# Scores of the output factor copied to SBUF before their maximum and exponential

## The chip, the cores and the metric

One NeuronCore of one Trainium2 chip runs one program. The metric is the time of the whole program on the device, in microseconds (us). Engines are named as the profile names them: PE is TensorE (its weight loads are PEld), DVE is VectorE, ACT is ScalarE, POOL is GpSimd, SP is SyncE, which issues the transfers.

## What is computed

Landmark (Nystrom) attention on 4 batches of 8 heads, 576 positions of 64, then two feed-forward layers on the 2304 rows that come out, one with the activation h*cos(h) and one with a leaky rectifier. Three soft maxima stand in the attention; the third, C (landmark queries against all keys), is what the change touches:

```
def sm(a, b):
    s = scale * np.matmul(a, b.transpose(0, 1, 3, 2))
    s = s - np.max(s, axis=-1, keepdims=True)
    e = np.exp(s)
    return e / (np.sum(e, axis=-1, keepdims=True) + 1e-09)
A = sm(q, k_lm)
Bm = sm(q_lm, k_lm)
C = sm(q_lm, k)
...
return (A @ Z @ C @ v).astype(np.float32)
```

## The kernel before, in words

The program has two parts. Up to about 485 us it does attention and the first layer, interleaved: `tick(s)` (128 of them) makes one tile of the first layer's hidden values for 128 hidden units and 288 rows, with six matmuls into a bank "h" (L949), a cosine on ACT and DVE (L954 to L963), and twelve matmuls into four banks "acc" (L976). Between them stand `unit(u)` (8 of them, two per batch, each 4 heads), which makes the soft maxima A and C, `z_path(b)`, which makes the inverse Z, `vprime` (L909), which multiplies Z C v by the first layer's weights, and `convert` (L471, L473, L475), which turns the weights from 64-bit to 32-bit numbers on DVE. From 485 us on the second layer runs (L1235, L1316).

PSUM has eight banks: two "h", two "x", four "acc". The units of batch 0 (m = 0) use "h", "x" and "acc" while no tick runs. The units of batches 1 to 3 (m = 1, u = 2 to 7) have only the two "x" banks for all that they do, and share them with `z_path` and `vprime`.

In such a unit the scores of C come in two pieces of 320 and 256 columns (L670). Both stay in their "x" banks while DVE takes a maximum of each (L685) and one of the two (L687), and until ACT has made the exponentials from there into SBUF with their sums (L692). Then PE transposes the result (L700, L704) and multiplies by v (L715). The scores of A come by the same L670 into "x" again, and DVE transposes them into SBUF (L742).

The order of all work is made by a planner when the program is built (class `Plan`): every operation has a cost, an estimated start and a due time, buffers have so many places, and each engine takes, one after the other, what can start next. Operations that two engines can do are given to the one that is free first. So an edit to one operation moves others on all engines. The lines:

Of the kernel before, what the change touches and what calls it, by code (L numbers as in the profile page):

```python
# [12 lines left out]
AF = mybir.ActivationFunctionType  # L13
ALU = mybir.AluOpType
# [244 lines left out]
def kernel(  # L259
# [12 lines left out]
    nc = tc.nc  # L272
# [63 lines left out]
    def lay(age, at, *items):  # L336
        for tag, n, size in items:
            place[tag] = (age, size, [at + i * size for i in range(n)])
            at += n * size
        return at  # L340

    at = lay(0, 0, ("f", 4, 4 * FW), ("wo", 8, 2048))
    at_va = at
    at = at_a = lay(0, at, ("va", 4, 4096))
    at = at_wi = lay(0, at, ("a", 8, 4 * S))
    at = at_wh = lay(0, at, ("wi", 8, 2048))
    at = at_raw = lay(0, at, ("wt", 4, 1024))
# [9 lines left out]
    def att(m, *items):  # L357
        return [(f"{m}{tag}", n, size) for tag, n, size in items]

    KT, ST = 4 * NR * P, [("cmx", 2, 16), ("cnm", 2, 16), ("csm", 2, 16), ("crs", 2, 16), ("amx", 2, 80), ("asm", 2, 80)]  # L360
    at_z = lay(1, at_1, *att(1, ("kt", 1, KT), ("qt", 2, KT), ("ce", 1, CE), ("at", 2, 4 * S), ("lt", 1, 256), *ST))
    at_0 = lay(0, at_w + 2048, *att(
        0, ("kn", 2, KT), ("qn", 2, KT), ("vn", 2, 4 * RAW), ("kt", 2, KT), ("qt", 2, KT),
        ("ktc", 1, KT), ("qtc", 1, KT), ("ce", 2, CE), ("ls", 4, 512), ("cet", 2, CE), ("at", 2, 4 * S), ("a2", 2, 4 * S),
# [52 lines left out]
    def psb(tag):  # L417
        return g.buf(tag, lambda _: ps.tile([P, 512], F32, tag=tag, name=tag, bufs=g.caps[tag]))
# [32 lines left out]
    def loads(n, fn, dur, r=(), w=(), target=None, after=(), rw=(), hold=()):  # L451
        return op(sp(n), fn, r=r, w=w, rw=rw, target=target, after=after, dma=dur, hold=hold)
# [66 lines left out]
            conv_wo(j)  # L519

    py, Cc = {}, {}
    wt, ah = {}, {}

    def atb(m, tag, shape):
        return sb(f"{m}{tag}", shape)

    def unit(u, tu):
# [37 lines left out]
        def ldv(e):  # L565
            for bb in range(2):
                src = v[b, 4 * c + 2 * bb:4 * c + 2 * bb + 2].rearrange("h (p r) d -> p h r d", r=NR)
                nc.sync.dma_start(out=vv_(vn)[0:64, bb], in_=src[:, :, 0:R0, :])
                nc.sync.dma_start(out=vv_(vn)[64:128, bb, :, 0:R1, :], in_=src[:, :, R0:NR, :])
        loads(4, ldv, 1.64, w=[vn], after=aft)  # L570
        gates["ld"] = aft

        T = {}
# [94 lines left out]
        def scores(dst, ch, which, t, bb, pp):  # L668
            n = 64 * (CH[ch][1] - CH[ch][0])
            nc.tensor.matmul(  # L670
                out=dst.t[64 * bb:64 * bb + 64, 0:n],
                lhsT=kq[pp][:, which, bb].rearrange("p h m -> p (h m)"),
                rhs=t.t[:, CH[ch][0]:CH[ch][1], bb, :],
            )

        sc = pair()
        mx, nm_, sm = atb(m, "cmx", [P, 2]), atb(m, "cnm", [P, 1]), atb(m, "csm", [P, 2])
        for ch in range(2):
            n = (N0, N1)[ch]
# [7 lines left out]
        op(dve(2), lambda e: nc.vector.tensor_reduce(nm_.t, mx.t, axis=AX.X, op=ALU.max, negate=True),  # L687
           r=[mx], w=[nm_])
        ce = atb(m, "ce", [P, R0, 2, 64])
        for ch in range(2):  # L690
            n = (N0, N1)[ch]
            op(("ACT", n / 1200.0 + 0.18), lambda e, ch=ch, n=n: nc.scalar.activation(  # L692
                ce.t[:, 0:n // 64, ch, :], sc[ch].t[:, 0:n].rearrange("p (r s) -> p r s", s=64),
                AF.Exp, bias=nm_.t, accum_out=sm.t[:, ch:ch + 1]), r=[sc[ch], nm_], w=[ce, sm], aset="exp")
# [6 lines left out]
        o1 = op(pe(512, 2), et1, r=[ce], w=[e1, et])  # L701
# [7 lines left out]
        def cv(e):  # L709
# [51 lines left out]
    def z_path(b, tz):  # L761
# [36 lines left out]
        vop(nm_, lambda e: nv.tensor_tensor(bm.t, pbv(), mx.t.to_broadcast([P, n, M]), op=ALU.subtract),  # L798
            r=[pb, mx], w=[bm])
# [582 lines left out]
```

## Time and profile before

| what | us |
|---|---|
| median of 3 runs | 882.39 (881.43 to 885.32) |
| the profiled execution | 881.18 |
| its span in the trace | 879.4 |
| mean granted TensorE clock | 0.984 of full speed |

The page gives the busy time of each engine over the span; since the program has two parts with different limits, the stretches of time are what to read, and within a stretch, which engine waits for which. All rows below come from the profiled execution, which lies 1.2 us below the median of the three runs.

### The profile page before, as it was taken

The numbers are of one execution on the slowest core, as the hardware profiler recorded it, in microseconds if no ns is written. First come the engines' busy times: TensorE is split into PE (matmuls) and PEld (weight loads), VectorE is DVE, ScalarE is ACT, GpSimd is POOL, SyncE is SP. The second block draws the span as 40 slices with busy tenths as digits, with TensorE's granted clock in tenths as the row PEclk, the third lists the DMA queues.
The fourth block names the chain that finished last, engine by engine and source line by source line (L and its number), as shares of the span: only waits on it lengthen the run. The fifth ranks groups of instructions, "written<-read, shape, count | busy, mean of one in ns | idle before, by whom it ended". The sixth has DMA issues, their size and how long they took to land.

```text
span 879.4 us, 15395 instructions
## 1 busy us (share of the span) xinstructions
PE 825.8 (94%) x5681; PEld 726.3 (83%) x5681; DVE 646.4 (74%) x1279; ACT 483.9 (55%) x1118; POOL 198.2 (23%) x220
## 2 busy tenths in 40 slices
PE   5677899999999998999989999999999999999997
PEld 4436789888798887897889888889999999999996
DVE  4989969987896889768998777775665566555563
ACT  4467757777875687667678534443344334333431
POOL 1224511333321332114432222200120012000110
PEclk8989999999999999999999999999999999999999
DMA  8476506775359846666555111140113011310231
GB/s 233 116 215 143 171 26 189 229 178 136 123 159 268 230 119 196 186 182 218 182 185 181 51 48 48 61 132 25 37 61 85 25 37 60 85 37 25 66 115 24
DMA packets 89051, 107.44 MB, mean 122 GB/s; under 512 B 35984, under 2 KB 63120, under 8 KB 88976
## 3 DMA queue, kind: packets, MB, share of 16 engines
q1 hardware_dynamic: 88976, 106.46, 41.2%
q8 instruction: 44, 0.72, 0.3%
q14 instruction: 31, 0.25, 0.1%
HBM read 82.06 MB, written 24.38 MB: 121 GB/s over the span
## 4 chain that ended last, share of the span: by engine, by line
PE 61%; DVE 19%; DMA 10%; issue 3%; ACT 3%; SPq 1%; POOL 1%; DVEq 0%; POOLq 0%; ACTq 0%
PE acc L1316 21%; PE acc L976 10%; PE h L1235 9%; PE x L1235 7%; PE h L949 5%; DMA m<-in_moe_w_in_dram 4%; DMA m<-in_moe_w_out_dram 3%; DVE m L323 3%; DVE m L475 3%; DVE m L473 3%; PE x L909 2%; DMA m<-wi2d 2%; DVE m L471 2%; DVE m L960 2%; DVE m L956 2%
## 5 line engine op out<-in xcount | busy, mean ns | idle before, releaser
L976 PE MATMUL acc<-m,m 128*128 128x288 f32 x1536 | 238.0, 301 | 7.0 <-DVE m L323 3.4
L323 POOL TENSOR_TENSOR m<-m,m 128x288 fp32r<-128x288 f32 (+3 forms) x129 | 126.0, 984 | 459.7 <-ACT m L963 233.5
L976 PEld LDWEIGHTS acc<-m,m 128*128 128x128 f32 x1536 | 213.7, 190 | 18.4 <-issue 7.7
L1316 PE MATMUL acc<-m,m 128*128 128x512 f32 x864 | 207.5, 392 | 0.7 <-DVE m L323 0.4
L323 DVE TENSOR_TENSOR m<-m,m 128x512 fp32r<-128x512 f32 (+4 forms) x271 | 170.3, 651 | 34.9 <-ACT m L1184 9.3
L1316 PEld LDWEIGHTS acc<-m,m 128*128 128x128 f32 x864 | 158.9, 189 | 31.9 <-DVE m L323 0.9
L949 PE MATMUL h<-m,m 128*128 128x288 f32 x768 | 131.8, 307 | 14.9 <-DVE m L960 12.8
L949 PEld LDWEIGHTS h<-m,m 128*128 128x128 f32 x768 | 109.6, 191 | 34.9 <-DVE m L960 19.9
L1304 ACT ACTIVATE m<-m 128x512 fp32r<-128x512 f32 (+1 forms) x80 | 46.3, 588 | 111.5 <-DVE m L1302 109.0
L1235 PE MATMUL h<-m,m 128*128 128x256 f32 x768 | 106.9, 282 | 0.7 <-ACT m L318 0.6
L1235 PEld LDWEIGHTS h<-m,m 128*128 128x128 f32 x768 | 99.7, 189 | 3.6 <-ACT m L318 1.3
L1258 DVE TENSOR_TENSOR m<-h,m 128x512 f32<-128x512 f32 x32 | 22.1, 690 | 81.8 <-ACT m L318 78.9
L1235 PE MATMUL x<-m,m 128*128 128x256 f32 x576 | 80.3, 283 | 1.7 <-ACT m L318 1.7
L963 ACT ACTIVATE m<-m 128x288 fp32r<-128x288 f32 x128 | 55.8, 441 | 40.5 <-DVE m L960 35.4
L1235 PEld LDWEIGHTS x<-m,m 128*128 128x128 f32 x576 | 73.1, 188 | 3.4 <-ACT m L318 1.9
L318 ACT ACTIVATE m<-h 128x256 f32<-128x256 f32 (+2 forms) x93 | 36.8, 396 | 67.2 <-PE h L1235 58.9
L958 ACT ACTIVATE m<-m 128x288 f32<-128x288 f32 x128 | 55.6, 440 | 26.4 <-DVE m L956 26.0
L960 DVE SCALAR_TENSOR_TENSOR m<-m,h 128x288 f32<-128x288 f32 x128 | 56.5, 446 | 15.1 <-ACT m L959 14.8
L1095 ACT ACTIVATE m<-m 128x512 fp32r<-128x512 f32 x68 | 41.4, 628 | 45.0 <-PE h L1235 19.4
L954 ACT ACTIVATE m<-h 128x288 int32<-128x288 f32 x128 | 51.4, 404 | 22.8 <-PE h L949 22.0
L956 DVE SCALAR_TENSOR_TENSOR m<-h,m 128x288 f32<-128x288 f32 x128 | 57.0, 448 | 3.4 <-ACT m L954 3.2
L959 ACT ACTIVATE m<-m 128x288 f32<-128x288 f32 x128 | 55.2, 439 | 2.4
(150 smaller groups left out, 897.5 us busy)
## 6 DMA issues: line engine op xcount, KB each, us to landing
m<-in_moe_w_in_dram SPq DMA_DIRECT2D x32, 512.0 KB, 5.4
m<-in_moe_w_out_dram SPq DMA_DIRECT2D x32, 512.0 KB, 4.4
m<-wi2d SPq DMA_DIRECT2D x56, 256.0 KB, 3.5
m<-w1d SPq DMA_DIRECT2D x32, 256.0 KB, 5.5
y1d<-m SPq DMA_DIRECT2D x24, 288.0 KB, 2.8
out_dram<-m SPq DMA_DIRECT2D x36, 128.0 KB, 2.4
w1d<-m SPq DMA_DIRECT2D x16, 256.0 KB, 5.3
wi2d<-m SPq DMA_DIRECT2D x16, 256.0 KB, 2.9
```

The costliest lines, as they stand in the source:

```text
L323: ENG[e].tensor_tensor(o, a, b, op=ALU.subtract)
L949: nc.tensor.matmul(out=hp.t[:, 0:CW], lhsT=w_[:, js], rhs=x[:, cs], start=(i == 0), stop=(i == 5))
L954: op(act(CW, True), lambda e: nc.scalar.activation(k_.t, hp.t[:, 0:CW], AF.Copy, scale=INV2PI), r=[hp], w=[k_], target=T + 0.8)
L956: op(dve(CW), lambda e: nc.vector.scalar_tensor_tensor(u.t, hp.t[:, 0:CW], INV2PI, k_.t, op0=ALU.mult, op1=ALU.subtract), r=[hp, k_], w=[u])
L958: op(act(CW), lambda e: nc.scalar.activation(u.t, u.t, AF.Sin, scale=math.pi), rw=[u], aset="sin")
L959: op(act(CW), lambda e: nc.scalar.activation(u.t, u.t, AF.Square, scale=math.sqrt(2.0)), rw=[u])
L960: op(dve(CW), lambda e: nc.vector.scalar_tensor_tensor(hc.t, u.t, 1.0, hp.t[:, 0:CW], op0=ALU.subtract, op1=ALU.mult, reverse0=True), r=[h ...
L963: op(act(CW), lambda e: nc.scalar.activation(gh.t, hc.t, AF.Copy), r=[hc], w=[gh, gl])
L976: nc.tensor.matmul(out=yg[o].t[:, 0:CW], lhsT=w_.t[:, sl], rhs=x.t, start=(j == ja and i == 0), stop=(j == jb and i == 2),)
L1235: nc.tensor.matmul(out=rv(k), lhsT=a_.t[:, p, c2, js], rhs=b_.t[:, q_, c2, 0:hw], start=(first and c2 == 0 and i == 0), stop=(c2 == 1 and ...
L1304: op(act(w), lambda e, m_=m_, gh=gh: nc.scalar.activation(gh.t[:, 0:w], m_.t[:, 0:w], AF.Copy), r=[m_], w=[gh, gl])
L1316: nc.tensor.matmul(out=ya[n][t].t, lhsT=gv(x_), rhs=r_.t, start=(st and k == 0), stop=(en and k == 2))
```

## The change

For batches 1 to 3 each piece of the scores is copied to SBUF as soon as it is there, by ACT or DVE, whichever the planner finds free; one maximum over all 576 columns (negated at once) and one exponential over all 576, in place, follow there. The two banks are no longer taken as a pair, neither for C nor, for the first piece, for A. The buffer of C (`1ce`) gets a second place; the room for it comes from `wt`, which goes from four places to two, and from smaller places for the small columns. Batch 0 stays as it was. The dictionary `marks` only keeps names of operations; nothing reads it.

```
-    at = at_raw = lay(0, at, ("wt", 4, 1024))
+    at = at_raw = lay(0, at, ("wt", 2, 1024), ("cex", 1, CE))
...
+    place["1ce"] = (1, CE, place["1ce"][2] + place.pop("cex")[2])
...
-        sc = pair()
-        mx, nm_, sm = atb(m, "cmx", [P, 2]), atb(m, "cnm", [P, 1]), atb(m, "csm", [P, 2])
+        sc = pair() if m == 0 else (psb("x"), psb("x"))
+        mx = None if m else atb(m, "cmx", [P, 2])
+        nm_, sm = atb(m, "cnm", [P, 1]), atb(m, "csm", [P, 2])
+        ce = None
...
+            if m:
+                ce = ce or atb(m, "ce", [P, R0, 2, 64])
+                op(pe(n, 4), cs, r=[kt, kqb[p][1]], w=[sc[ch]])
+                op([act(n, True), dve(n)], lambda e, ch=ch, n=n: copy(
+                    e, ce.t[:, 0:n // 64, ch, :], sc[ch].t[:, 0:n].rearrange("p (r s) -> p r s", s=64)),
+                   r=[sc[ch]], w=[ce])
+                continue
...
+        if m:
+            def ces():
+                return ce.t.rearrange("p r t s -> p (r t s)")[:, 0:S]
+            marks["cn", b, c] = op(dve(S), lambda e: nc.vector.tensor_reduce(
+                nm_.t, ces(), axis=AX.X, op=ALU.max, negate=True), r=[ce], w=[nm_])
+            marks["ce", b, c] = op(("ACT", S / 1200.0 + 0.18), lambda e: nc.scalar.activation(
+                ces(), ces(), AF.Exp, bias=nm_.t, accum_out=sm.t[:, 0:1]), r=[nm_], rw=[ce], w=[sm], aset="exp")
...
+        if m:
+            op(dve(2), lambda e: nc.vector.tensor_scalar_add(rs.t[:, 0:1], sm.t[:, 0:1], 1e-9), r=[sm], w=[rs])
...
-               w=[sa[ch]] if ch else [*sa, at], after=[o1] if ch else [])
+               w=[sa[ch]] if ch else [sa[ch], at] if m else [*sa, at], after=[o1] if ch else [])
```

How the order of the instructions moves is shown at three places. In the rows of the changed kernel the lines of the old steps are 2 to 23 higher (L954 is L977, L956 L979, L960 L983, L963 L986, L670 L672, L700 L719, L704 L723, L715 L734, L976 L999, and L471, L473, L475 are L473, L475, L477).

In these rows m_ and a number is a place in SBUF, and x, h and acc are banks of PSUM.

DVE, first unit of batch 3 (u = 6), from the conversion ahead of the maxima on. Before:

```order
L471 TENSOR_SCALAR m_573<-m_157 128x512
L323 TENSOR_TENSOR m_504<-m_479,m_504 128x288
L473 SCALAR_TENSOR_TENSOR m_573<-m_157,m_573 128x512
L685 TENSOR_REDUCE m_69<-x 128x1 x2
L475 SCALAR_TENSOR_TENSOR m_573<-m_157,m_573 128x512
L687 TENSOR_REDUCE m_69<-m_69 128x1
L956 SCALAR_TENSOR_TENSOR m_479<-h,m_479 128x288
L471 TENSOR_SCALAR m_420<-m_157 128x512
L473 SCALAR_TENSOR_TENSOR m_420<-m_157,m_420 128x512
L475 SCALAR_TENSOR_TENSOR m_420<-m_157,m_420 128x512
L723 SCALAR_TENSOR_TENSOR m_69<-m_69 128x1
L725 RECIPROCAL m_69<-m_69 128x1
```

Now:

```order
L473 TENSOR_SCALAR m_574<-m_157 128x512
L323 TENSOR_TENSOR m_505<-m_480,m_505 128x288
L475 SCALAR_TENSOR_TENSOR m_574<-m_157,m_574 128x512
L477 SCALAR_TENSOR_TENSOR m_574<-m_157,m_574 128x512
L701 TENSOR_REDUCE m_69<-m_175 128x1
L979 SCALAR_TENSOR_TENSOR m_480<-h,m_480 128x288
L473 TENSOR_SCALAR m_421<-m_157 128x512
L764 STREAM_TRANSPOSE m_69<-x 128x320
L475 SCALAR_TENSOR_TENSOR m_421<-m_157,m_421 128x512
L764 STREAM_TRANSPOSE m_69<-x 128x256
L477 SCALAR_TENSOR_TENSOR m_421<-m_157,m_421 128x512
L743 TENSOR_SCALAR m_69<-m_69 128x1
```

The two maxima from the bank x and the small one of the two (L685, L687) are gone, and one maximum from SBUF (L701) stands behind the conversion instead of inside it; the transposes of A's scores (L764) come up ahead of the next conversion's end.

ACT, the same unit, around the exponentials. Before:

```order
L954 ACTIVATE m_479<-h 128x288
L663 ACTIVATE m_69<-m_69 64x2x32 x2
L692 ACT_TABLE_LOAD
L692 ACTIVATE m_175,m_69<-x,m_69 128x5x64
L692 ACTIVATE m_175,m_69<-x,m_69 128x4x64
L954 ACTIVATE m_479<-h 128x288
L958 ACT_TABLE_LOAD
```

Now:

```order
L986 ACTIVATE m_505<-m_480 128x288
L318 ACTIVATE m_175<-x 128x5x64
L318 ACTIVATE m_175<-x 128x4x64
L977 ACTIVATE m_480<-h 128x288
L665 ACTIVATE m_69<-m_69 64x2x32 x2
L703 ACT_TABLE_LOAD
L703 ACTIVATE m_175,m_69<-m_175,m_69 128x576
L977 ACTIVATE m_480<-h 128x288
L981 ACT_TABLE_LOAD
```

Two copies out of x (L318) come first, then the small scalings of the landmarks (L665), and one exponential in place (L703) behind the same table load.

PE, second unit of batch 3 (u = 7), from the transposes of C to its product with v. Before:

```order
L976 MATMUL acc<-m_504,m_1795 128x288 x3
L700 MATMUL x<-m_69,m_175 128x128 x4
L976 MATMUL acc<-m_504,m_1795 128x288 x6
L704 MATMUL x<-m_69,m_175 64x128
L976 MATMUL acc<-m_504,m_1795 128x288 x6
L670 MATMUL x<-m_175,m_69 64x320 x2
L670 MATMUL x<-m_175,m_69 64x256 x2
L976 MATMUL acc<-m_504,m_1795 128x288 x6
L715 MATMUL x<-m_157 32x64 x20
```

Now:

```order
L672 MATMUL x<-m_175,m_69 64x320 x2
L719 MATMUL x<-m_69,m_433 128x128 x4
L999 MATMUL acc<-m_505,m_1791 128x288 x6
L723 MATMUL x<-m_69,m_433 64x128
L999 MATMUL acc<-m_505,m_1791 128x288 x3
L672 MATMUL x<-m_175,m_69 64x256 x2
L999 MATMUL acc<-m_505,m_1791 128x288 x3
L734 MATMUL x<-m_157 32x64 x20
```

The first piece of A's scores (L672, 320 columns) stands ahead of the transposes of C (L719, L723) now, and 12 matmuls into acc instead of 18 stand between these transposes and the product with v (L734).

## Rows read from the trace of the kernel before

**Rows 1.** The page, first part: busy us of each engine, share of span, instructions.
```profile
PE 825.8 (94%) x5681; PEld 726.3 (83%) x5681; DVE 646.4 (74%) x1279; ACT 483.9 (55%) x1118; POOL 198.2 (23%) x220
```

**Rows 2.** Stretches: length; busy (instructions) of PE, PEld, DVE, ACT, POOL; clock; DMA; GB/s.
```profile
50.00:130.00 80.00, 66.31 (x482) 52.81 (x482) 66.92 (x144) 51.03 (x119) 28.61 (x29) 0.94 0.51 137
...
192.00:256.00 64.00, 62.61 (x521) 54.05 (x521) 52.65 (x132) 52.86 (x118) 22.46 (x30) 1.00 0.48 131
...
294.00:366.00 72.00, 68.19 (x551) 58.29 (x552) 62.77 (x142) 54.09 (x125) 24.12 (x32) 1.00 0.56 158
...
485.00:880.00 395.00, 386.18 (x2422) 348.68 (x2420) 242.11 (x415) 149.72 (x323) 52.51 (x51) 0.99 0.19 57
```

**Rows 3.** Waits of PE, 50 to 366 us: total, times, longest.
```profile
PE h L949 <- DVE m L960: 6.7, 11, 3.6
...
PE x L700 <- ACT m L692: 1.5, 1, 1.5
```

**Rows 4.** DVE groups by form, 50 to 366 us: busy, mean ns, idle before.
```profile
L747 DVE TENSOR_REDUCE m<-m 128x18 f32<-128x576 f32 x6 | 4.5, 748 | 0.1
...
L685 DVE TENSOR_REDUCE m<-x 128x1 f32<-128x320 f32 x6 | 2.9, 486 | 0.9 <-PE x L670 0.8
...
L685 DVE TENSOR_REDUCE m<-x 128x1 f32<-128x256 f32 x6 | 2.5, 414 | 0.0
...
L687 DVE TENSOR_REDUCE m<-m 128x1 f32<-128x2 f32 x6 | 0.9, 143 | 0.0
```

**Rows 5.** The same view, operations that either engine can do (last row: 0 to 485).
```profile
L320 DVE COPY m<-x 128x384 f32<-128x384 f32 x5 | 2.8, 555 | 2.3 <-PE x L594 2.2
...
L320 DVE COPY m<-x 128x512 f32<-128x512 f32 x2 | 1.4, 681 | 0.0
...
L320 DVE COPY m<-m 32x64 f32<-32x64 f32 x6 | 1.1, 181 | 0.1
...
L323 DVE TENSOR_TENSOR m<-m,m 128x288 fp32r<-128x288 f32 x60 | 34.9, 587 | 7.0 <-ACT m L963 5.6
```

**Rows 6.** ACT groups by form, 50 to 366 us.
```profile
L318 ACT ACTIVATE m<-x 128x384 f32<-128x384 f32 x28 | 12.9, 488 | 2.7 <-PE x L594 2.5
...
L749 ACT ACTIVATE m<-m 128x576 f32<-128x576 f32 x6 | 4.1, 683 | 0.1
...
L692 ACT ACTIVATE m<-x,m 128x320 f32<-128x320 f32 x6 | 3.2, 527 | 0.1
L692 ACT ACTIVATE m<-x,m 128x256 f32<-128x256 f32 x6 | 2.8, 467 | 0.0
```

**Rows 7.** First unit of batch 3: chain (first row), DVE and ACT in time order.
```profile
304.55 1.12 PE x L670 x8
...
306.62 0.82 DVE L685 TENSOR_REDUCE m<-x 128x1 f32<-128x320 f32 x2
...
306.70 0.41 ACT L954 ACTIVATE m<-h 128x288 int32<-128x288 f32 x1 [2.06 <-PE h L949]
...
307.52 1.28 ACT L692 ACT_TABLE_LOAD   x1
308.81 0.53 ACT L692 ACTIVATE m<-x,m 128x320 f32<-128x320 f32 x1
...
309.69 0.20 ACT L692 ACTIVATION_READ_ACCUMULATOR m<-x,m 128x1 f32 x1
```

**Rows 8.** Waits of DVE, 50 to 366 us: total, times, longest.
```profile
DVE m L471 <- DMA m<-in_moe_w_in_dram: 7.1, 6, 2.4
...
DVE m L742 <- PE x L670: 2.3, 3, 1.2
...
DVE m L750 <- ACT m L749: 1.5, 1, 1.5
...
DVE m L723 <- ACT m L692: 1.3, 2, 0.6
...
DVE m L685 <- PE x L670: 0.8, 2, 0.5
```

More of the change, by code (lines that the diff above doesn't have):

```diff
@@ L340, in lay @@
         return at
+    CE = 4 * R0 * P
     at = lay(0, 0, ("f", 4, 4 * FW), ("wo", 8, 2048))
@@ L346 @@
     at = at_wh = lay(0, at, ("wi", 8, 2048))
-    at = at_raw = lay(0, at, ("wt", 4, 1024))
-    CE = 4 * R0 * P
+    at = at_raw = lay(0, at, ("wt", 2, 1024), ("cex", 1, CE))
     at = lay(0, at, ("raw", 3, 4 * RAW))
@@ L360 @@
     KT, ST = 4 * NR * P, [("cmx", 2, 16), ("cnm", 2, 16), ("csm", 2, 16), ("crs", 2, 16), ("amx", 2, 80), ("asm", 2, 80)]
-    at_z = lay(1, at_1, *att(1, ("kt", 1, KT), ("qt", 2, KT), ("ce", 1, CE), ("at", 2, 4 * S), ("lt", 1, 256), *ST))
+    ST1 = [("cnm", 2, 8), ("csm", 2, 8), ("crs", 2, 8), ("amx", 2, 72), ("asm", 2, 72)]
+    at_z = lay(1, at_1, *att(1, ("kt", 1, KT), ("qt", 2, KT), ("ce", 1, CE), ("at", 2, 4 * S), ("lt", 1, 256), *ST1))
     at_0 = lay(0, at_w + 2048, *att(
@@ L521 @@
     py, Cc = {}, {}
-    wt, ah = {}, {}
+    wt, ah, marks = {}, {}, {}
     def atb(m, tag, shape):
@@ L569, in ldv @@
                 nc.sync.dma_start(out=vv_(vn)[64:128, bb, :, 0:R1, :], in_=src[:, :, R0:NR, :])
-        loads(4, ldv, 1.64, w=[vn], after=aft)
+        marks["vl", b, c] = loads(4, ldv, 1.64, w=[vn], after=aft)
         gates["ld"] = aft
@@ L686, in unit @@
                r=[sc[ch]], w=[mx])
[L687 to L694, printed above, removed]
+        if m:
[5 more added lines that the diff above has]
+                ces(), ces(), AF.Exp, bias=nm_.t, accum_out=sm.t[:, 0:1]), r=[nm_], rw=[ce], w=[sm], aset="exp")
+        else:
+            op(dve(2), lambda e: nc.vector.tensor_reduce(nm_.t, mx.t, axis=AX.X, op=ALU.max, negate=True),
+               r=[mx], w=[nm_])
+            ce = atb(m, "ce", [P, R0, 2, 64])
+            for ch in range(2):
+                n = (N0, N1)[ch]
+                op(("ACT", n / 1200.0 + 0.18), lambda e, ch=ch, n=n: nc.scalar.activation(
+                    ce.t[:, 0:n // 64, ch, :], sc[ch].t[:, 0:n].rearrange("p (r s) -> p r s", s=64),
+                    AF.Exp, bias=nm_.t, accum_out=sm.t[:, ch:ch + 1]), r=[sc[ch], nm_], w=[ce, sm], aset="exp")
         e1, e2 = bank(0), bank(1)
@@ L700, in et1 @@
                 nc.tensor.transpose(e1.t[:, r * P:(r + 1) * P], ce.t[:, r].rearrange("p t s -> p (t s)"), ident)
-        o1 = op(pe(512, 2), et1, r=[ce], w=[e1, et])
+        o1 = marks["et", b, c] = op(pe(512, 2), et1, r=[ce], w=[e1, et])
         op([act(512), dve(512)], lambda e: copy(e, et.t[:, 0:R1].rearrange("p r m -> p (r m)"), e1.t),
@@ L722, in unit @@
         rs = atb(m, "crs", [P, 2])
-        op(dve(2), lambda e: nc.vector.scalar_tensor_tensor(
-            rs.t[:, 0:1], sm.t[:, 0:1], 1e-9, sm.t[:, 1:2], op0=ALU.add, op1=ALU.add), r=[sm], w=[rs])
+        if m:
+            op(dve(2), lambda e: nc.vector.tensor_scalar_add(rs.t[:, 0:1], sm.t[:, 0:1], 1e-9), r=[sm], w=[rs])
+        else:
+            op(dve(2), lambda e: nc.vector.scalar_tensor_tensor(
+                rs.t[:, 0:1], sm.t[:, 0:1], 1e-9, sm.t[:, 1:2], op0=ALU.add, op1=ALU.add), r=[sm], w=[rs])
         op(dve(2), lambda e: nc.vector.reciprocal(rs.t[:, 1:2], rs.t[:, 0:1]), rw=[rs])
@@ L747, in unit @@
         op(dve(S), lambda e, mxa=mxa, at=at: nc.vector.reduce_max(mxa.t, at.t, axis=AX.X), r=[at], w=[mxa])
-        op(tt, lambda e, mxa=mxa, at=at: sub(e, at.t, at.t, mxa.t.to_broadcast([P, NBK, M])), r=[mxa], rw=[at])
-        op(act(S), lambda e, at=at: nc.scalar.activation(at.t, at.t, AF.Exp), rw=[at], aset="exp")
+        marks["as", b, c] = op(tt, lambda e, mxa=mxa, at=at: sub(
+            e, at.t, at.t, mxa.t.to_broadcast([P, NBK, M])), r=[mxa], rw=[at])
+        marks["ae", b, c] = op(act(S), lambda e, at=at: nc.scalar.activation(at.t, at.t, AF.Exp), rw=[at], aset="exp")
         op(dve(S), lambda e, sma=sma, at=at: nc.vector.reduce_sum(sma.t, at.t, axis=AX.X), r=[at], w=[sma])
@@ L797, in z_path @@
         vop(nm_, lambda e: nv.reduce_max(mx.t, pbv(), axis=AX.X), r=[pb], w=[mx])
-        vop(nm_, lambda e: nv.tensor_tensor(bm.t, pbv(), mx.t.to_broadcast([P, n, M]), op=ALU.subtract),
-            r=[pb, mx], w=[bm])
+        marks["zs", b] = op(dve(nm_), lambda e: nv.tensor_tensor(
+            bm.t, pbv(), mx.t.to_broadcast([P, n, M]), op=ALU.subtract), r=[pb, mx], w=[bm])
         op(act(nm_), lambda e: nc.scalar.activation(bm.t, bm.t, AF.Exp, scale=8.0), rw=[bm], aset="exp")
```

## The prediction

> **What bounds the kernel now.** I read four views, from coarse to fine. The page's first part [rows 1] shows PE busy for 94% of the span; that alone would say that work of DVE and ACT is free. The table by stretches [rows 2] says otherwise, and it is the view to read here. From 485 us on PE is busy 386.18 of 395 us: nothing there waits for the units, and the change alters nothing in it. The units that the change touches stand in three earlier stretches: batch 1 at 50 to 130 us, batch 2 at 192 to 256, batch 3 at 294 to 366. In each, PE loses time (13.7, 1.4 and 3.8 us idle), and DVE is busy 66.92 of 80, 52.65 of 64 and 62.77 of 72 us: 82 to 87%, which leaves little for waits in one queue that takes its work in order. So I take DVE as what sets the pace there. The waits of PE over 50 to 366 us [rows 3] fit: the longest is PE at a tick's first matmuls for L960, a DVE step (6.7 us in 11 waits). Of the changed steps PE has waited for the exponential (L692) once, 1.5 us. No wait of PE names a bank; a bank that is late shows as a wait for whoever reads it last.
>
> **DVE's work.** Six units change. Out go twelve maxima from PSUM: 2.9 us for the six of 320 columns, 2.5 for the six of 256; and six small maxima of the two, 0.9 [rows 4]. In come six maxima over 576 columns from SBUF. The trace has that operation in another place: L747, a maximum over 576 fp32 columns from SBUF, 4.5 us for six. The new one has one output column in place of 18; I take the same price. The small addition after it (one operand in place of two) takes the place of L723 and is priced as it. Of the twelve copies the order gives eleven to ACT and one of 256 columns to DVE; between a maximum over as many PSUM columns (0.41 us [rows 4]) and a copy of 384 (0.56 [rows 5]) I take 0.43, near the first, which has the same size. Sum: 4.5 + 0.4 - 5.4 - 0.9 = -1.4 us.
>
> The planner also shifts work that either engine can do. Counted over both orders DVE loses five copies of 32x64, one of 128x384 and one subtraction of 128x288, and gains two copies of 128x512: by rows 5, -0.91 - 0.56 - 0.59 + 1.36 = -0.7 us. (One small copy goes and one small scaling comes; I set them against each other.) DVE has 2.1 us less to do in all. With DVE busy 85% of these stretches, 0.85 x 2.1 = 1.8 us of it lies on the path. Bounds: 0, if what is saved only lengthens DVE's waits, and -2.1.
>
> The Trainium skill speaks against this part: Perfetto Trace Analysis, Optimizing Scalar/DVE Operations, says that long operations pay where the engine is saturated, and that where it only causes bubbles elsewhere, broken-up work may finish sooner. By the same section's overheads of an instruction on DVE (some 125 ns on PSUM, 60 on SBUF) I would estimate that one maximum saves 2 x 125 - 60 = 190 ns against two, 1.1 us over six units; rows 4 give 0.9. Which half of the rule holds hangs on whether DVE is saturated; 85% is nearer to saturated, so by it the sum stands, and by its other half the first rival below comes true.
>
> **ACT's work.** Out: twelve exponentials, 3.2 + 2.8 us, with a read of the accumulator of 0.20 behind each, 2.4 us [rows 6, 7]. In: six exponentials over 576 columns at 0.68 (L749's price) with a read each, 5.3 us, and eleven copies of 256 or 320 columns, for which I take 0.44, somewhat under the 0.49 that 384 take, 4.8 us. That is +1.7 us; the table loads stay as many. ACT is busy 51 to 54 us in stretches of 64 to 80 [rows 2], so I cost this at nothing: the cover is DVE, which has more to do. If the cover were gone, at most +1.7.
>
> **The chain inside a unit.** In the first unit of batch 3 the scores begin at 304.55, the first maximum starts at 306.62, the last exponential's read ends at 309.89 [rows 7]: both banks are held for over 5 us. Of this the changed work is 0.82 (maxima), 0.14 for the small one [rows 4], and 1.08 (exponentials); the table load of 1.28 overlaps part of it and stays. Now: the copies end some 0.5 us after the last score, the maximum takes 0.75, the exponential with its read 0.88. That is 2.0 before and 2.1 now. The chain does not get shorter; what gets shorter is the time for which the banks are held, from 5 us to about 1.5. PE has no matmul more or less. The second place of `1ce` takes a wait away that no row shows; the two places of `wt` that go cost nothing, since a batch's tile is used up (last by its L909) long before the batch after next needs the place. No transfer is added; SP's order shifts by a few loads around the units, and I cost that at nothing, with the longest wait of DVE for such weights, 2.4 us [rows 8], as the bound either way.
>
> **Sum.** -1.8 us against the profiled execution's 881.18. That execution lies 1.2 us below the median of the runs, and a median is what will be measured, so I set the sum against 882.4: **880.6 us**. About 0.5%, 4.4 us, is what a measurement of this kernel can tell from no change; the forecast is below that.
>
> **Rivals.**
>
> 1. *A new wait on ACT.* Until now DVE took a maximum as soon as PE had a piece ready. Now PE hands to ACT and ACT to DVE, and in DVE's queue the long maximum stands ahead of ticks' steps (L960) for which PE waits. If DVE gets there before the copies have landed, it stands still for a copy (0.4 us) and for what ACT has ahead of it: between nothing and a table load of 1.28 [rows 7]. Taking the middle, 1.1 us for each of six units: +6.6, with the 1.8 less that is +4.8, **887.2 us**. For it: DVE was already there too early for scores in two maxima and three transposes (0.8 and 2.3 us [rows 8]). Against it: the order now puts the maximum behind a whole conversion, and ACT stood idle for 2.1 us just ahead of the unit's exponentials [rows 7]. It decides if DVE waits for L318 ahead of L701 by over 4 us in total.
>
> 2. *Early banks set the units free.* With the banks held for 1.5 us, A's scores come earlier (in the second unit of batch 3 their first piece has moved ahead of C's transposes), and DVE's waits inside the units go: L742 for L670 2.3 us, L750 for L749 1.5, L723 for L692 1.3, L685 for L670 0.8 [rows 8], 5.9 us in all. With the 1.8 that is -7.7: **874.7 us**. Against it: these are waits in a queue that has other work, and what stands behind moves up to the next wait (that for the weights' transfers is the next, 7.1 us [rows 8]). The Trainium skill is on this rival's side: PSUM — Partial Sum Buffer, Summary: rules for kernel authors, says to evacuate promptly because the memory is tight. Rows 3 show little waiting for it.
>
> 3. *It does not do what it says.* The copies stand in queues in order; where they wait there, the banks come free no sooner, and only the 1.8 us remains, eaten by ACT's +1.7: **882.4 us**.
>
> **How the numbers follow.** Forecast 0.43, first rival 0.22, second 0.25, third 0.10. The forecast's bounds and the third rival lie within 4.4 us of 882.4 but for tails, which the reshuffled order gives both: 0.03 to faster, 0.03 to slower. So faster 0.28, same 0.47, slower 0.25. The range takes in the forecast with its bounds, about half of the second rival (874.7 lies just outside, 0.13 left out) and two thirds of the first (0.07 left out): 875.0 to 888.0.
>
> **What would show it.** Right: in the three stretches DVE's busy sum falls by about 2 us (182.3 now [rows 2]) and ACT's rises by 1 to 2; L701 reads 0.75 us; PE's matmuls from 485 us on are as long as before; the tick waits of PE for L960 stay near 6.7 us. The first rival shows as DVE waits for L318 and longer PE waits for L960, the second as missing waits at L742, L750 and L723 and a second layer that starts 6 us sooner. Wrong is the forecast if the start of the second layer moves by over 4 us either way, above all if it moves though DVE's sum in the stretches is the one forecast: then the order, and not the work, has decided.

## The result: slower by 0.7%

The changed kernel takes 889.04 us (median of 13 runs, 885.53 to 891.97) against 882.39 (13 runs, 879.70 to 886.28): a ratio of 1.0067, with a 95% interval of 1.0045 to 1.0089. The forecast was 880.6, with 875.0 to 888.0 as its range. The two profiled executions, 885.60 and 881.18 us, lie 4.4 us apart and not 6.7, since that of the changed kernel is one of its shorter runs; the tables below are made from them, so they hold some two thirds of the loss.

First the work. The page of the changed kernel, its first part:

```profile
PE 826.2 (93%) x5681; PEld 726.4 (82%) x5681; DVE 645.0 (73%) x1263; ACT 487.4 (55%) x1121; POOL 196.3 (22%) x221
```

Against [rows 1] PE is the same, DVE has 1.4 us less, ACT 3.5 more. The same stretches as in [rows 2], with PE, PEld, DVE, ACT and POOL in this order:

```profile
50.00:130.00 80.00, 66.82 (x477) 53.90 (x477) 66.72 (x142) 54.16 (x120) 24.37 (x26) 0.89 0.51 137
192.00:256.00 64.00, 62.65 (x523) 53.58 (x522) 51.34 (x126) 50.86 (x112) 19.82 (x28) 1.00 0.48 132
294.00:366.00 72.00, 70.09 (x569) 59.76 (x566) 61.40 (x138) 57.74 (x135) 25.67 (x33) 1.00 0.63 173
```

DVE's sum is 179.5 us, 2.9 less than the 182.3 of before. ACT's is 162.8, 4.8 more than the 158.0 of before, where 1 to 2 were forecast. The changed kernel is late in these stretches, so they do not hold quite the same work; cut at the same ticks (below), DVE's sum falls by 2.3 us and ACT's rises by 3.3. Either way DVE has less to do. The groups by form, DVE and then ACT, 50 to 370 us, answer to [rows 4, 6]:

```profile
L701 DVE TENSOR_REDUCE m<-m 128x1 f32<-128x576 f32 x6 | 4.5, 749 | 1.2 <-ACT m L318 1.0
...
L703 ACT ACTIVATE m<-m,m 128x576 f32<-128x576 f32 x6 | 4.7, 776 | 0.1
```

The new maximum takes 749 ns, the price taken for it was 748; the exponential in place takes 776 and not 680. The first unit of batch 3, chain, DVE and ACT in time order, as in [rows 7]:

```profile
311.86 0.76 PE L672 MATMUL x<-m,m 128*64 128x320 f32 x4
...
312.67 0.44 ACT L318 ACTIVATE m<-x 128x320 f32<-128x320 f32 x1 [0.26 <-PE x L672]
...
313.14 0.65 PE L672 MATMUL x<-m,m 128*64 128x256 f32 x4
...
313.84 0.39 ACT L318 ACTIVATE m<-x 128x256 f32<-128x256 f32 x1 [0.73 <-PE x L672]
...
314.45 0.74 DVE L701 TENSOR_REDUCE m<-m 128x1 f32<-128x576 f32 x1
```

From the first score to the end of its copy a bank is held for 1.25 us (311.86 to 313.11), the other for 1.1. Before, the first was held for 4.8 us (304.55 to the end of its exponential, 308.81 plus 0.53) and the second, taken together with it, for over 5. The change does what it says.

**Where the time goes.** In the trace a tick begins with the first of six matmuls of L949 (L972 now); there are 768 of them, six for each of 128 ticks. Between the same ticks the two kernels do nearly the same work, so I cut both traces at ticks 0, 22, 40, 64, 88 and 127. Before:

```profile
47.00:143.40 96.40, 81.82 (x587) 66.40 (x586) 81.71 (x174) 63.37 (x151) 29.69 (x30) 0.95 0.49 134
143.40:191.90 48.50, 46.76 (x326) 42.12 (x325) 46.67 (x90) 35.12 (x90) 15.64 (x13) 1.00 0.68 205
191.90:276.30 84.40, 82.84 (x664) 72.49 (x664) 68.43 (x166) 65.52 (x149) 26.18 (x34) 1.00 0.57 164
276.30:366.60 90.30, 85.33 (x663) 72.71 (x663) 75.01 (x169) 63.87 (x148) 25.73 (x34) 1.00 0.64 176
366.60:478.90 112.30, 106.04 (x736) 97.07 (x735) 93.09 (x175) 79.54 (x202) 37.73 (x39) 0.98 0.62 205
```

Now:

```profile
47.20:143.90 96.70, 83.23 (x581) 67.37 (x580) 80.87 (x172) 66.08 (x152) 26.52 (x28) 0.91 0.48 132
143.90:198.20 54.30, 48.59 (x338) 43.61 (x337) 48.88 (x89) 36.64 (x93) 17.88 (x16) 1.00 0.67 200
198.20:286.10 87.90, 84.33 (x660) 73.12 (x659) 69.95 (x162) 63.87 (x146) 24.91 (x33) 0.98 0.50 148
286.10:370.60 84.50, 82.59 (x660) 71.66 (x659) 70.64 (x156) 64.99 (x152) 27.53 (x35) 1.00 0.67 183
370.60:485.00 114.40, 105.70 (x740) 96.25 (x740) 92.31 (x177) 79.18 (x201) 37.32 (x39) 1.00 0.63 204
```

The first window holds batch 1's units and is 0.3 us longer; the fourth, with those of batch 3, is 5.8 shorter. The loss is in the second (+5.8), the third (+3.5) and the last (+2.1); a second trace of the changed kernel (e9 below) has +6.0, +1.6 and +2.9 there. The second is the one to look at first: no changed step runs between ticks 22 and 40, and it is where DVE was fullest, 46.67 of 48.5 us. There DVE has one instruction fewer, yet is busy 2.2 us longer and PE waits more. PE's and DVE's waits there, before:

```profile
PE h L949 <- DVE m L960: 1.1, 3, 0.6
PE h L949 <- DVE m L912: 0.5, 1, 0.5
...
DVE m L471 <- DMA m<-in_moe_w_in_dram: 1.3, 2, 0.8
DVE m L471 <- DMA m<-in_moe_w_out_dram: 0.4, 1, 0.4
```

and now:

```profile
PE h L972 <- DVE m L983: 5.7, 6, 1.6
...
DVE m L473 <- DMA m<-in_moe_w_in_dram: 2.2, 3, 1.4
DVE m L473 <- DMA m<-in_moe_w_out_dram: 1.8, 1, 1.8
```

One place shows how. DVE of the changed kernel at tick 28, and PE behind it:

```profile
159.57 0.68 DVE L477 SCALAR_TENSOR_TENSOR m<-m,m 128x512 int32<-128x512 int32 x1
162.07 0.43 DVE L473 TENSOR_SCALAR m<-m 128x512 int32<-128x512 int32 x1 [1.82 <-DMA m<-in_moe_w_out_dram]
162.53 0.69 DVE L475 SCALAR_TENSOR_TENSOR m<-m,m 128x512 int32<-128x512 int32 x1
163.14 0.45 DVE L979 SCALAR_TENSOR_TENSOR m<-h,m 128x288 f32<-128x288 f32 x1
163.51 0.44 DVE L983 SCALAR_TENSOR_TENSOR m<-m,h 128x288 f32<-128x288 f32 x1
...
164.01 1.07 PE L972 MATMUL h<-m,m 128*128 128x288 f32 x6 [1.61 <-DVE m L983]
```

A weight conversion's first two steps (L473, L475) stand ahead of the steps of two ticks. Its weights have not landed, DVE stands still for 1.82 us, L983 comes late, and PE waits 1.61 us for it. In the kernel before the same conversion stands behind the steps of both ticks, and DVE waits 0.38 us for it:

```profile
159.30 0.44 DVE L960 SCALAR_TENSOR_TENSOR m<-m,h 128x288 f32<-128x288 f32 x1
159.66 0.44 DVE L956 SCALAR_TENSOR_TENSOR m<-h,m 128x288 f32<-128x288 f32 x1
160.49 0.43 DVE L471 TENSOR_SCALAR m<-m 128x512 int32<-128x512 int32 x1 [0.38 <-DMA m<-in_moe_w_out_dram]
```

None of these is a changed step: behind batch 1, where the changed steps are planned otherwise, the planner puts the rest elsewhere too.

The third window has the same picture at one place, with the clock behind it. DVE and PE in time order, then the stretch from 278 us:

```profile
275.17 0.43 DVE L473 TENSOR_SCALAR m<-m 128x512 int32<-128x512 int32 x1 [2.70 <-DMA m<-in_moe_w_in_dram]
...
276.02 1.06 PE L972 MATMUL h<-m,m 128*128 128x288 f32 x6 [2.11 <-DVE m L983]
...
278.31 1.64 PE L972 MATMUL h<-m,m 128*128 128x288 f32 x6
...
278.00:280.00 2.00, 2.00 (x11) 2.00 (x10) 1.13 (x3) 0.90 (x3) 0.00 (x0) 0.50 1.01 350
```

DVE stands still for 2.70 us for weights ahead of L983, and PE waits 2.11 us for that step. Right behind this pause the granted clock falls from 1.00 to 0.72 of full speed in the mean of 276 to 282 us, with 0.50, the lower of its two levels (1.2 GHz), at 278 to 280; six matmuls of L972 take 1.64 us there and 1.06 just before. The wait and the clock (6 us at 0.72, some 1.7 us by my estimate) together are about the 3.5 us that this window loses. In e9, where it loses 1.6, the clock of the window reads 1.00.

### The profile page after: what moved, and what is told of

Its sections match the earlier page's. It is cut to its first block, busy times and chain, and to the rows that moved or that the text cites. A ratio compares the mean times of both kernels' runs of the same rounds, so it can differ in the third digit from the quotient of the medians.

```text
span 883.8 us, 15379 instructions
## 1 busy us (share of the span) xinstructions
PE 826.2 (93%) x5681; PEld 726.4 (82%) x5681; DVE 645.0 (73%) x1263; ACT 487.4 (55%) x1121; POOL 196.3 (22%) x221
## 4 chain that ended last, share of the span: by engine, by line
PE 64%; DVE 16%; DMA 9%; ACT 4%; issue 4%; SPq 1%; POOL 1%; DVEq 0%; POOLq 0%; ACTq 0%
PE acc L1339 20%; PE acc L999 12%; PE h L1258 9%; PE x L1258 7%; PE h L972 6%; DMA m<-in_moe_w_in_dram 4%; DVE m L323 3%; DVE m L475 2%; DMA m<-in_moe_w_out_dram 2%; PE x L932 2%; DVE m L477 2%; DMA m<-wi2d 2%; DVE m L473 2%; DVE m L979 2%; DVE m L983 1%
## 5 line engine op out<-in xcount | busy, mean ns | idle before, releaser
L999 PE MATMUL acc<-m,m 128*128 128x288 f32 x1536 | 237.6, 301 | 4.4 <-ACT m L457 1.9
L999 PEld LDWEIGHTS acc<-m,m 128*128 128x128 f32 x1536 | 214.3, 190 | 15.4 <-issue 7.6
L323 DVE TENSOR_TENSOR m<-m,m 128x512 fp32r<-128x512 f32 (+4 forms) x270 | 167.7, 643 | 34.3 <-ACT m L1207 9.0
L972 PE MATMUL h<-m,m 128*128 128x288 f32 x768 | 134.5, 311 | 17.5 <-DVE m L983 16.4
L972 PEld LDWEIGHTS h<-m,m 128*128 128x128 f32 x768 | 111.4, 194 | 38.8 <-DVE m L983 22.4
L986 ACT ACTIVATE m<-m 128x288 fp32r<-128x288 f32 x128 | 56.1, 441 | 46.8 <-DVE m L983 43.9
L318 ACT ACTIVATE m<-h 128x256 f32<-128x256 f32 (+2 forms) x93 | 36.9, 397 | 66.2 <-PE h L1258 58.1
L983 DVE SCALAR_TENSOR_TENSOR m<-m,h 128x288 f32<-128x288 f32 x128 | 57.0, 446 | 15.0 <-ACT m L982 14.9
L977 ACT ACTIVATE m<-h 128x288 int32<-128x288 f32 x128 | 51.7, 404 | 24.6 <-PE h L972 23.8
L979 DVE SCALAR_TENSOR_TENSOR m<-h,m 128x288 f32<-128x288 f32 x128 | 57.3, 449 | 6.0 <-ACT m L977 5.6
```

The costliest lines, as they stand in the source:

```text
L972: nc.tensor.matmul(out=hp.t[:, 0:CW], lhsT=w_[:, js], rhs=x[:, cs], start=(i == 0), stop=(i == 5))
L977: op(act(CW, True), lambda e: nc.scalar.activation(k_.t, hp.t[:, 0:CW], AF.Copy, scale=INV2PI), r=[hp], w=[k_], target=T + 0.8)
L979: op(dve(CW), lambda e: nc.vector.scalar_tensor_tensor(u.t, hp.t[:, 0:CW], INV2PI, k_.t, op0=ALU.mult, op1=ALU.subtract), r=[hp, k_], w=[u])
L983: op(dve(CW), lambda e: nc.vector.scalar_tensor_tensor(hc.t, u.t, 1.0, hp.t[:, 0:CW], op0=ALU.subtract, op1=ALU.mult, reverse0=True), r=[h ...
L986: op(act(CW), lambda e: nc.scalar.activation(gh.t, hc.t, AF.Copy), r=[hc], w=[gh, gl])
L999: nc.tensor.matmul(out=yg[o].t[:, 0:CW], lhsT=w_.t[:, sl], rhs=x.t, start=(j == ja and i == 0), stop=(j == jb and i == 2),)
```

## The experiments

**Theory "order"**: the changed steps are worth about the forecast's sum, and the reshuffled queues cost the rest. **Theory "steps"**: copies, a longer chain through ACT, and steps in place cost it, and the order only shows it. To part them I made the planner's order something that can be carried over: each step has a name (its context and its number there) that both kernels share, and the list of steps with their engines, as the planner put them out, is written into the kernel and followed.

```diff
+        todo = {}
+        for e, rank, key in ORDER:
+            todo.setdefault(e, []).append((rank, key))
         while left:
             best = None
-            for e, lst in ready.items():
+            if any(todo.values()):
...
+                            sl = None if o is None else slots(o)
+                            if sl is None:
+                                continue
...
+                            if best is None or rank < best[0]:
+                                best = (rank, d, o, s, e)
...
+                todo[best[4]].remove((best[0], best[2].key[2]))
+            for e, lst in () if best else ready.items():
```

In a kernel with this list the lines behind it are some 270 higher than in the changed kernel (L1244 is its L972, L949 in the kernel before; L1255 its L983, L960 before). The list holds a step's place and its engine together, so the runs do not part these two; "order" below means both. All medians and ratios stand in the table at the end of this section.

**e1: the new steps in the old order.** Seven steps of a unit become six where they stood:

```diff
-scores0 max0 scores1 max1 small_max exp0 exp1
+scores0 copy0 scores1 copy1 max exp
```

> The changed steps (copies, one maximum, one exponential, the new places in SBUF, banks singly) in the order of the kernel before on all five queues; a copy stands where a maximum stood, the long maximum where the small one stood, the exponential where the first one stood. Theory 'order' (the planner's reshuffled queues cost the 6 us, the steps themselves are worth about what the sum said): 879 to 883 us, ratio 0.996 to 1.001. Theory 'steps' (the copies and the chain through ACT and DVE cost it): 887 to 890, ratio 1.006 or more.

Measured: 880.28 us, ratio 0.9975 (0.9957 to 0.9993). "Steps" is out: in the old order the new steps are faster than the old ones by 2.2 us (0.6 to 3.8), and the forecast's sum was 1.8. The new places in SBUF are in this kernel too, so they do not cost the loss either. Most of the waits that the second rival wanted to see gone are still there; in DVE's waits, 50 to 366 us, the transpose of A's scores (L1036 here) and the sum behind the exponential of A (L1045) read

```profile
DVE m L1036 <- PE x L944: 2.0, 3, 1.2
DVE m L1045 <- ACT m L1044: 1.5, 1, 1.5
```

against 2.3 and 1.5 in [rows 8].

**e2: the old steps in the new order**, the same in the other direction.

> The converse: the old steps (two maxima, a small one, two exponentials, banks in pairs, old places) in the order of the changed kernel; 16 pairs of neighbours among some 4,160 steps swap where a bank is not yet free. Theory 'order': 887 to 891 us, ratio 1.005 to 1.010, with the second layer late as in the changed kernel. Theory 'steps': 881 to 884.

Measured: 893.98 us, ratio 1.0122 (1.0095 to 1.0149), beyond what either theory said. The order costs 1.2% with the old steps; with the new ones the step from 0.9975 to 1.0067 is 0.9% (0.75% to the 1.0050 of e9). In this order too the new steps are the better ones, 1.0067 against 1.0122. But it was planned for the new steps: here 6.1 of the 12.5 us are lost before tick 22, among the units of batch 1, where the changed kernel loses 0.5. So e2 shows that this order is a bad one for the old steps, not that it loses at the same places.

**e3: the changed kernel with SP's queue in the old order.**

> The changed kernel with SP's queue (all transfers) in the order of the kernel before; the other four queues as in the changed kernel. If the loss comes from the order of the transfers (DVE's waits for weights between the units 4.0 us against 1.8): 882 to 885 us, ratio 1.000 to 1.003. If it comes from what stands where on DVE and PE: 887 to 890, ratio 1.005 or more. Theory 'steps': 887 to 890 too.

Measured: 899.1 us, ratio 1.0197 (1.0163 to 1.0231), a miss: beyond the times of both branches. In ticks 22 to 40 it loses 6.2 us, as much as the changed kernel, so the loss there is not due to the order of the transfers alone. Some 11.4 more are lost in ticks 52 to 58, where one row of DVE's waits (251 to 280 us; L744 is L471) has the reason:

```profile
DVE m L744 <- DMA m<-in_moe_w_in_dram: 9.1, 2, 5.2
```

Here an order of transfers belongs to the order of the queue that uses them; half of one and half of the other is worse than either.

**e4: the old order up to tick 64, the changed kernel's from there.**

```diff
-ORDER: changed kernel, ticks 0 to 128 and the second layer
+ORDER: kernel before to tick 64; changed kernel behind it
```

> The changed steps, in the order of the kernel before up to tick 64 (233 us of the plan, 250 us of the trace), and from there in the order of the changed kernel. Theory 'order', with the loss in ticks 8 to 64 (+9.8 us at tick 64) and a gain in batch 3 (-5.9 from tick 64 to tick 88): 876 to 881 us, ratio 0.993 to 0.999. If the loss is one that follows whatever stands before, or the gain was only the catching up of a late PE: 882 to 886. Theory 'steps': 887 to 890.

Measured: 878.85 us, ratio 0.9961 (0.9941 to 0.9981), inside the range of "order" with a place. The trace has it nearly as expected: -1.4 us at tick 40, -0.9 at 64, -5.9 at 88, so a gain of 5.1 from 64 to 88 where 5.9 was expected. That e4 beats e1 is not shown, the intervals overlap.

**e5: that kernel with ticks 22 to 40 in the changed order**, the window by itself.

> The fourth run's kernel (changed steps, old order to tick 64) with one window more in the changed order: ticks 22 to 40 of every queue. If that window's order costs its 5.8 us by itself: ratio to the kernel before 1.001 to 1.005 (0.9961 without it), with PE waiting for L960's step 5 us there and tick 40 some 4 to 6 us later than in the fourth run. If the 5.8 us hang on what stood before the window, or are given back behind it: ratio 0.995 to 0.998.

Measured: 0.9983 (0.9963 to 1.0003), 0.2% over e4 and between the two branches; the intervals of the two overlap, so by the times alone no cost of the window is shown. In the trace it costs 3.8 us (from -0.9 at tick 22 to +2.9 at tick 40, against nothing in e4), PE waits 4.5 us for L983's step there, and e5 is 3.3 us behind e4 at tick 127. So by one trace of each the window's order does cost by itself, but some 3 to 4 us rather than 5.8. Ticks 22 to 40 of e4, then of e5:

```profile
142.00:190.50 48.50, 46.52 (x326) 42.11 (x325) 46.50 (x90) 35.06 (x90) 15.53 (x13) 1.00 0.69 202
142.46:194.82 52.36, 47.69 (x333) 42.83 (x332) 49.16 (x89) 36.40 (x93) 17.50 (x16) 1.00 0.71 206
```

DVE is busy 2.7 us longer with one instruction fewer, as it is in the changed kernel (2.2 us), while POOL has 16 instructions in place of 13. DVE's waits for weights are only 1.4 us here, less than the 1.7 of the kernel before. So late weights are not needed for the loss; DVE's longer work, on which the last section has more, is the greater part of it in e5.

**e10: the converse, the changed kernel with ticks 22 to 40 in the old order.**

> The changed kernel with one window, ticks 22 to 40 of every queue, in the order of the kernel before; all else as changed. If the 5.8 us of that window are its order's own: 3 to 6 us under the ninth run of the same chip, ratio 0.999 to 1.004, tick 40 at most 1.5 us later than before. If they hang on the state in which the window is reached: within 2 us of the ninth run.

Measured: 885.75 us, 2.6 under the changed kernel's 888.36 on the same chip (ratio 1.0025, 1.0006 to 1.0044): between the two branches, and the intervals of the two ratios overlap. In the trace the gain is whole up to tick 37: +1.2 us against the +6.4 of e9. Then most of it goes, for a reason that is new. PE's waits, 145 to 196 us:

```profile
PE x L868 <- DMA m<-in_q_dram: 2.3, 1, 2.3
PE h L1244 <- DVE m L1255: 1.1, 1, 1.1
```

The waits for L983's step are down to 1.1, as in the kernel before, and PE comes to the transposes of q of batch 2 before q has landed: tick 40 is at +4.5.

**e6: four DVE steps moved up**, L983 of ticks 22, 27, 31 and 35, each ahead of the last one or two steps of a conversion. At tick 27:

```diff
+L983 (tick 27)
 L473 (conversion 20)
 L475 (conversion 20)
 L979 (tick 28)
-L983 (tick 27)
```

> The changed kernel with four DVE steps moved up and nothing else: in ticks 22, 27, 31 and 35 the step of L983 goes ahead of the one or two steps of a weight conversion that stood before it. If PE's waits for L983 in ticks 22 to 40 (5.7 us in 6) come from those steps of conversion standing ahead: waits of PE there under 3 us, ratio to the kernel before 1.002 to 1.005 in place of 1.0067. If DVE is short of time there as a whole (it then only waits for the same weights a step later): 1.006 to 1.008.

Measured: ratio 1.0032 (1.0009 to 1.0054), but on another chip than the changed kernel's 1.0067; **e9** ran the changed kernel again to settle that.

> The changed kernel once more, unaltered, beside the next three on one chip, and with a second trace. The sixth run's ratio (1.0032 with four moves) was taken on another chip than the changed kernel's 1.0067. If the four moves gained what their ratio says: this comes out at 1.005 or more, with PE waiting longer for L983 in ticks 22 to 40 than the sixth run's 5.0 us. If the sixth run's trace is right (tick 40 only 0.5 us earlier) and the rest is a difference between chips: 1.002 to 1.005.

Measured: 888.36 us, 1.0050 (1.0031 to 1.0069), and PE's waits for L983 there are 4.6 us. The two intervals overlap, so no gain of the four moves is shown. The trace of e6 shows what became of the waits; those of PE and DVE, 143.5 to 197.7 us (L1241, L1252 and L742 are L972, L983 and L473, and L1251 is the step of ACT ahead of L983):

```profile
PE h L1241 <- DVE m L1252: 4.9, 8, 1.5
...
DVE m L1252 <- ACT m L1251: 2.5, 3, 1.3
...
DVE m L742 <- DMA m<-in_moe_w_in_dram: 0.9, 2, 0.5
```

DVE's waits for weights fall from 4.0 to 0.9 us, and a wait for ACT takes their place: at its new place L983 comes before ACT has its operand ready. My guess that the conversions in front of L983 are the whole cause is wrong; here, where DVE has 46.67 of 48.5 us to do, the steps moved away from one wait landed in the next. Which of the moved steps of the window would have to go back stays open.

**e7, e11, e12: a reshuffle with nothing of the change in it.** The kernel before, where only the planner's price of a DVE step is altered:

```diff
-        return ("DVE", n / 960.0 + 0.07)
+        return ("DVE", n / 960.0 + 0.071)
```

and 0.069 and 0.072. This moves 241, 184 and 242 steps on DVE, where the change moves 244.

> The kernel before, nothing of the change in it; the planner's price of a DVE step is 0.001 us higher, which moves 241 steps on DVE and 16 on SP against the order before (the change moves 244 and 19). It measures what a reshuffle costs by itself. Theory 'order', with orders differing by chance about a tuned one: outside 0.997 to 1.003, slower likelier, about 1.005 to 1.015. If a reshuffle of this size is harmless by itself: 0.998 to 1.002.

> The kernel before with the planner's price of a DVE step 0.001 us lower: 184 steps move on DVE, 11 on SP. A second draw of a reshuffle without the change, after 1.0011 for the first. If draws spread by half a per cent or more: outside 0.998 to 1.002; if a reshuffle of this size is worth less than the change's order (e2: 1.012 with the old steps): 0.998 to 1.004.

> The same with the price 0.002 us higher: 242 steps move on DVE, 15 on SP. A third draw; as for the eleventh run.

Measured: 1.0011 (0.9991 to 1.0030), 1.0070 (1.0041 to 1.0098) and 1.0059 (1.0035 to 1.0082). Two of three cost as much as the change. The first costs nothing that can be measured and so falls into the branch that spoke against "order": a reshuffle of this size can be harmless. With the change's own order (e2) that is four other orders for the same steps, and none is better than the one before.

**e8: the best windows put together**, with the new steps: old order to tick 64, new in 64 to 88, old in 88 to 128, new in the second layer.

> The changed steps; order of the kernel before to tick 64, of the changed kernel in ticks 64 to 88 (which gained 4.5 us in the fourth run), of the kernel before in ticks 88 to 128 (the fourth run lost 2.2 there), of the changed kernel in the second layer (gained 1.5). If windows add up: 876 to 878 us, ratio 0.992 to 0.995. If what a window gains hangs on what follows it: like the fourth run, 0.996, or worse.

Measured: 878.95 us, ratio 0.9939 (0.9916 to 0.9962): faster than both kernels, with the ratio in the first branch and the median just above it. That it also beats e4 is not shown, the intervals overlap.

The whole on one page: medians, ratios, and the start of a tick against that of the kernel before, in us (one trace each; the last column is the end of the span).

| kernel | median us | ratio | 22 | 40 | 64 | 88 | 127 | end |
|---|---|---|---|---|---|---|---|---|
| before, from the span's start | 882.39 | | 143.4 | 191.9 | 276.3 | 366.6 | 478.9 | 879.4 |
| changed | 889.04 | 1.0067 | +0.5 | +6.3 | +9.8 | +3.9 | +6.1 | +4.4 |
| e9, changed again | 888.36 | 1.0050 | +0.9 | +6.9 | +8.5 | +2.8 | +5.7 | +5.6 |
| e1, new steps, old order | 880.28 | 0.9975 | +0.8 | +1.0 | +0.7 | +1.5 | +1.5 | +1.3 |
| e2, old steps, new order | 893.98 | 1.0122 | +6.1 | +10.4 | +14.3 | +10.9 | +14.1 | +12.5 |
| e3, old order on SP alone | 899.10 | 1.0197 | +3.9 | +10.1 | +20.1 | +17.9 | +21.4 | +21.2 |
| e4, old order to tick 64 | 878.85 | 0.9961 | -1.4 | -1.4 | -0.9 | -5.9 | -3.7 | -5.2 |
| e5, e4 with new 22 to 40 | 882.23 | 0.9983 | -0.9 | +2.9 | +3.1 | -1.7 | -0.4 | -0.6 |
| e10, changed with old 22 to 40 | 885.75 | 1.0025 | +1.7 | +4.5 | +7.3 | +2.9 | +5.6 | +5.5 |
| e6, changed, four moves | 886.39 | 1.0032 | +0.2 | +5.8 | +9.3 | +3.4 | +5.7 | +4.0 |
| e7, before, price 0.071 | 884.75 | 1.0011 | +1.7 | +3.0 | +0.7 | +1.1 | +2.3 | +0.6 |
| e11, before, price 0.069 | 889.92 | 1.0070 | +3.9 | +6.8 | +8.3 | +5.8 | +7.7 | +7.7 |
| e12, before, price 0.072 | 888.82 | 1.0059 | +3.8 | +5.1 | +5.9 | +5.6 | +6.4 | +6.3 |
| e8, best windows | 878.95 | 0.9939 | +1.1 | +1.0 | +1.5 | -1.8 | -0.3 | -2.1 |

One trace of each is read here, and two traces of the changed kernel (its own and e9's) differ by up to 1.4 us at one tick; differences of that size in the table mean nothing. The spread is understated by this pair: single runs of the changed kernel lie between 885.53 and 891.97 us, and the execution traced can lie well off the median, 2.2 us above it in e1 and 2.9 below it in e4. So e1's +1.3 at the end stands beside a median that is lower than before, and the ratios decide. They are of several runs each, against those of the kernel before on the same chip.

## Why the prediction was wrong

**The sum is not contradicted.** -1.4 us for DVE's changed steps and -1.8 on the path was the forecast, the latter with a third from the planner's shifts; with the order held (e1), and so without these shifts, the steps gain 2.2 us (0.6 to 3.8). The new maximum reads what L747 reads, and the bank's hold falls to 1.25 us where about 1.5 was said. That the gain comes the way the sum says is not shown: in e1's trace DVE is busy 641.5 us against 646.4, and 3.9 of these 4.9 us are in the three steps of the conversions (133.2 against 137.1), which the edit does not touch. ACT's rise in the stretches was undersized (+4.8 against +1 to 2, +3.3 by ticks; of this 0.6 us is the exponential's 776 ns in place of 680), and it cost nothing that e1 shows.

**The step that failed is the planner's shifts.** The prediction priced the reshuffle by which steps change their engine (-0.7 us) and SP's order at nothing, with 2.4 us as the bound. The runs show 6.6 to 8 us in place of -0.7: with the same new steps the ratio goes from 0.9975 in the old order to 1.0050 (e9) and 1.0067 in that of the change. Two things were missing. What stands ahead of what was not priced: the bound was a single wait of one queue, where ticks 22 to 40 alone have four waits for weights, six waits of PE and the steps behind them. And a step was taken at the same price whatever its neighbours: with three more subtractions on POOL there, DVE is busy 2.2 us longer (2.7 in e5). How the 6.6 to 8 us divide between the two is not shown, since every list carries places and engines together.

**The stretches left out the fullest one.** I read [rows 2] only where changed steps stand, and took DVE's 82 to 87% there for the sign that DVE sets the pace. Between them, from tick 22 to tick 40, DVE was 96% busy (46.67 of 48.5) with PE waiting 1.6 us in all: the tightest of the five windows, with no changed step in it, and every reshuffle in the table that begins before it passes through it. From tick 22 to 40 the changed order loses 5.8, e2 4.3, e3 6.2, and the three nudges (e7, e11, e12) 1.2, 2.9 and 1.3; kernels with the old order there lose at most 0.2 up to tick 37. It is not the only place, though: e2 and the nudges lose more before tick 22 (6.1, 1.7, 3.9 and 3.8), and putting the window back (e10) returns 2.6 us of the change's loss. That the rest falls before tick 64 is shown by e4; where, the trace alone says (the third window above).

**The rivals.** The first was right in sign and near in size (887.2) by luck, for a reason that is not there: DVE waits for L318 ahead of L701 once, 1.0 us, where over 4 was asked. In the changed kernel's waits of DVE, 50 to 366 us:

```profile
DVE m L473 <- DMA m<-in_moe_w_in_dram: 8.0, 7, 2.7
...
DVE m L773 <- ACT m L772: 4.0, 3, 1.6
...
DVE m L764 <- PE x L672: 1.1, 3, 0.5
DVE m L701 <- ACT m L318: 1.0, 1, 1.0
```

The waits for the exponential of A (L773) grow from 1.5 to 4.0 us, those for A's scores (L764) fall from 2.3 to 1.1: [rows 8] is only dealt anew. The second rival, early banks, wanted 7.7 us; at the same order (e1) the whole edit gains 2.2. What batch 3 gains in ticks 64 to 88 belongs mostly to the order: 5.9 us in the changed kernel, 3.4 in e2 with the old steps and banks, and a loss of 0.8 in e1 with the new ones in the old order. The Trainium skill's advice to evacuate promptly (PSUM — Partial Sum Buffer, Summary: rules for kernel authors) is followed by the change; no run here shows a gain that can be put down to it. Of the two halves of the rule that spoke against the change (the Trainium skill, Perfetto Trace Analysis, Optimizing Scalar/DVE Operations), the one on saturated engines is not contradicted by e1, whose edit as a whole gains; no run here has the long maximum by itself.

The forecast named its own falsifier, that the second layer starts over 4 us off while DVE's sum in the stretches is as said: "then the order, and not the work, has decided". That is what the trace shows (+6.1 us at tick 127, DVE's sum -2.9), and e1 and e4 confirm it. What was missing is a case for it among the rivals, with a chance of its own.

## What to carry to other kernels

Where a planner or scheduler sets the order of the queues, an edit of a few steps is also a fresh draw of the order everywhere behind it. Price that draw as a case by itself and with a spread, and read for it the stretches without an edited step too, the fullest first: here four other orders of the same steps came out at +0.1, +0.6, +0.7 and +1.2% (the last planned for other steps), three of them more than the edit is worth. To learn what an edit does, run it in the old order first; to keep its gain, carry the old order over, or put the better windows of both together, whole and with all queues (e4, e8). One queue of one order and four of the other was the worst of all here (e3).

## What was not expected of the hardware

A weight conversion's step on DVE has no fixed price. In the changed kernel, DVE and POOL in time order:

```profile
168.72 0.68 DVE L477 SCALAR_TENSOR_TENSOR m<-m,m 128x512 int32<-128x512 int32 x1
168.99 1.07 POOL L323 TENSOR_TENSOR m<-m,m 128x288 fp32r<-128x288 f32 x1 [2.18 <-ACT m L986]
169.32 1.29 DVE L475 SCALAR_TENSOR_TENSOR m<-m,m 128x512 int32<-128x512 int32 x1
170.53 0.44 DVE L983 SCALAR_TENSOR_TENSOR m<-m,h 128x288 f32<-128x288 f32 x1
```

L475 takes 1.29 us here beside POOL's subtraction; over all 64 of them the median is 1.17 us where POOL works during at least 30% of it (23 times) and 0.68 where not. L983, with one operand from PSUM, stays at 0.44 to 0.45 in the median either way. So even the sum of DVE's work hangs on the order: what a step costs depends on which engine the planner gives the neighbouring subtraction to. In ticks 22 to 40 conversions and subtractions of DVE take some 7 us more than their undisturbed durations (0.43 and 0.69 us for the steps of a conversion), some 6 in the kernel before, with 16 subtractions on POOL in place of 13. The Trainium skill (SBUF — State Buffer, Who interferes with whom) says that a DVE instruction with two inputs in SBUF contends with a GpSimd instruction that reads SBUF. The trace agrees, by the 1.17 against 0.68 us above.
